# A gate's mask in the tile of the gates' sums, and the parts of paired token operands in another order

## The chip, the cores and the metric

The kernel runs on one core of a Trainium2 chip. Its time is the device time of one execution, in microseconds (us). The engines are named as in the profile: PE is TensorE (PEld its weight loads), DVE is VectorE, ACT is ScalarE, POOL is GpSimd, SP is SyncE, which here only issues DMAs. All engines run side by side, each through its own list of instructions in a fixed order; semaphores make one wait for another.

## The reference

Attention with mixed heads, and behind it a feed-forward whose gate is `h - tanh(h)`:

```python
# q, k, v: (8, 12, 448, 64)   w_pre, w_post: (12, 12)   w_in: (768, 2048)   w_out: (2048, 768)
scores = scale * np.matmul(q, k.transpose(0, 1, 3, 2))
scores = np.einsum('bhij,hg->bgij', scores, w_pre)
scores = scores - np.max(scores, axis=-1, keepdims=True)
attn = np.exp(scores)
attn = attn / (np.sum(attn, axis=-1, keepdims=True) + 1e-09)
attn = np.einsum('bhij,hg->bgij', attn, w_post)
x = np.matmul(attn, v).transpose(0, 2, 1, 3).reshape(3584, 768)
h = x @ w_in
g = h - np.tanh(h)
out = g @ w_out
```

## The kernel before

The first half, up to about 880 us, is the attention, batch by batch, with its output `xs` stored to DRAM. The change does not touch it. The second half is the feed-forward on 3584 tokens in seven blocks of 512 (`TB`). To keep fp32 precision, each operand is split into a high part (a copy rounded to a shorter type, on ACT) and a low part (the operand less its high part, on DVE), and each product is three matmuls: high by high, high by low, low by high.

**Block 0** is computed plainly. `Block0.step` is called 18 times, f = 0 to 17. Each of the first 16 makes one tile of 128 features of h in a PSUM bank, by 18 matmuls (lines 285, 286, 288), and copies the bank to SBUF (ACT, line 347). Every two steps one `Gate` is computed for two feature tiles.

**The gate.** `Gate` computes h − tanh(h) twice and picks one by a mask, so that small h keep their precision. On ACT: a1 (lines 301 and 302: u = h², and a square for a polynomial, into the work tile qa), a2 (line 306: tanh into t; line 307: another square into qb), a3 (line 317: the Relu of u − 0.25, which is the mask, over qb). On DVE: d1 (line 310 makes qa further, line 311 makes t = h − tanh h), d2 (line 314: qa from qb and qa), d3 (line 320: the polynomial's result into the tile ga or gb), d4 (line 323, copy_predicated: t over that result where the mask is not zero). The tiles u, qa, qb, t, ga, gb, gs and the two h tiles (h01, h23) come from a pool with one buffer for each tag: who writes a tag again waits for all that read or write it before, DMAs included.

**Three paired stages** follow, each on two blocks of tokens at once, by a scheme of seven products in place of eight (Strassen and Winograd). `pair_step` is called 8 times a stage (24 in all). Each step makes seven products of nine matmuls, in the order b11, b21, t2, t1, t3, b22, t4, where the names are those of the token operands: quarters of the two blocks' inputs (b11, b21, b22) or sums of quarters (t1 to t4). The products go in turn to two PSUM banks, X and Y. Of X, ACT empties the first result by line 677, before the third product (t2) overwrites X; others are emptied by lines 683, 692, 700, 704, 712 and 718. At the end of a step the first gate (g1) gets its a1, a2, d1, d2 and a3; its d3 and d4, and the whole second gate (g2), are done in the next step by `Late`, cut into v0 to v5 between the products. `Late` also makes the sums of gates that the second matmul wants: v4 allocates the tile gs (three planes of 512 tokens) and adds into it (line 652), v5 adds the third plane and one of gb (lines 655 and 656), and then POOL stores gb and gs to DRAM (lines 657 and 658; line 635 stores ga). Between these pieces stand units of `Results`, the second matmul: for these, stored gates are loaded again (gl), cast (ACT, line 437) and made into low parts (DVE, line 443), and lines 495 to 497 (block 0) and 525 to 527 (paired blocks) multiply them by w_out.

**The parts of the token operands** are made by `xq_jobs`, a generator of eleven jobs for a stage: `sub` is a DVE subtraction of a 128x1536 tile (line 565), `high` an ACT copy (line 569), `low` a DVE subtraction (line 572), `both` the last two of a quarter in place. All sums are made in the one tile xr. In block 0 `between0(f)` runs one job in each of the steps f = 6, 8 and 10 to 15; what is left goes into the first paired step, one job behind each product. Between stages the list `jobs` in the tail runs all eleven among units of the second matmul: 16 or 14 held back from the stage and 2 or 4 ahead.

**Order.** `in_order` fixes on each engine the order in which the program is written; no scheduler moves anything.

Of the kernel before, what the change touches and what calls it, by code (L numbers as in the profile page):

```python
# [12 lines left out]
I32 = mybir.dt.int32  # L13
U32 = mybir.dt.uint32
AF = mybir.ActivationFunctionType
# [6 lines left out]
def raw(ap):  # L22

    return ap.bitcast(F32)
# [126 lines left out]
def kernel_body(  # L151
# [11 lines left out]
    nc = tc.nc  # L163
# [15 lines left out]
    scale = 1.0 / float(D) ** 0.5  # L179
    NK = DM // P  # L180
    NF = DF // P
# [39 lines left out]
    ff = SimpleNamespace(w={}, x={}, xs={}, wa={}, w2={}, gr={}, gp={})  # L221

    def pool(name, bufs, side, stack=ctx):
        return stack.enter_context(tc.tile_pool(name=name, bufs=bufs, side=side, reuse_waits="tile"))
# [15 lines left out]
    def rest_of_line(stack):  # L240

        pad = stack.enter_context(tc.tile_pool(name="pad", bufs=1, side="right"))
        nc.gpsimd.memset(pad.tile([P, LINE - 8], F32, name="pad", tag="pad"), 0.0)

    def open_late():
        rest_of_line(ctx)
        ff.xqb, ff.ca = pool("xqb", 1, "right"), pool("ca", 3, "right")
        ff.ps_y = ctx.enter_context(tc.tile_pool(name="ps_y", bufs=1, space=PSUM, side="left"))
# [5 lines left out]
    def work(tag, n=2):  # L254
        return ff.rw.tile([P, n, TB], F32, name=tag, tag=tag)
# [38 lines left out]
    class Gate:  # L294
# [19 lines left out]
            nc.vector.scalar_tensor_tensor(out=self.qa, in0=self.qb, scalar=GATE_B[2], in1=self.qa, op0=ALU.add, op1=ALU.mult)  # L314

        def a3(self):
            nc.scalar.activation(self.qb, self.u, AF.Relu, bias=ff.bias[:, 2:3], scale=1.0)

        def d3(self, out):
            nc.vector.tensor_mul(out, self.qa, self.u)  # L320

        def d4(self, out):
            nc.vector.copy_predicated(out, self.qb.bitcast(I32), self.t)


    class Block0:
# [36 lines left out]
    class Results:  # L363
# [65 lines left out]
        def high(self, n):  # L429
            if self.n_high <= n < len(self.items):  # L430
                self.n_high += 1
                if self.lead and n % (len(IDLE) + 2) < len(IDLE):
                    hi = work(IDLE[n % (len(IDLE) + 2)]).bitcast(F32R)
                else:
                    hi = ff.gph.tile([P, 2, TB], F32R, name="gh", tag="gh")
                ff.gp[n] = hi, ff.gr.pop(n)
                nc.scalar.copy(hi, raw(ff.gp[n][1]))  # L437

        def low(self, n):
            if self.n_low <= n < len(self.items):  # L440
                self.n_low += 1
                hi, lo = ff.gp[n]
                nc.vector.tensor_sub(lo, raw(lo), raw(hi))  # L443
# [106 lines left out]
    def x_tiles(*names):  # L550
        for x in names:
            p = ff.xqa if x == "t4l" else ff.xqb
            ff.xs[x] = p.tile([P, HK, TB], F32R, name=x, tag=x)
# [8 lines left out]
    def xq_jobs():  # L562

        def sub(x, y):
            nc.vector.tensor_sub(xr, x if x is xr else raw(ff.xs[x]), y if y is xr else raw(ff.xs[y]))

        def high(x, src):
            x_tiles(x + "h")
            nc.scalar.copy(ff.xs[x + "h"], src)

        def low(x, src):
            nc.vector.tensor_sub(ff.xs[x + "l"], src, raw(ff.xs[x + "h"]))

        def both(x):
            high(x, raw(ff.xs[x + "l"]))
            low(x, raw(ff.xs[x + "l"]))

        xr = ff.xr.tile([P, HK, TB], F32, name="xr", tag="xr")
        sub("t3l", "b11l")
        yield  # L580
        both("b11")
        yield
        x_tiles("t1l")
        high("t1", xr)
        low("t1", xr)
        yield
        sub("b22l", xr)
        yield
        x_tiles("t2l")
        high("t2", xr)  # L590
        low("t2", xr)
        yield
        sub("b21l", xr)
        yield
        x_tiles("t4l")
        high("t4", xr)
        low("t4", xr)
        yield
        both("b21")
        yield  # L600
        sub("b22l", "t3l")
        yield
        high("t3", xr)
        low("t3", xr)
        yield
        both("b22")
        yield

    IDLE = ("u", "qa", "qb", "t", "h01", "h23")
# [114 lines left out]
    with ExitStack() as st:  # L724
# [295 lines left out]
        def now(*engines):  # L1020
            place[0] += 1
            engines = engines or (nc.sync,)
            for x in (queue, slow):
                while x:
                    send(x, engines[len(x) % len(engines)])
# [43 lines left out]
        for w in range(2):  # L1069
            for at in AT[w]:  # L1070
                x = repeat[:, w, at : at + HP].rearrange("p (i h) -> p i h", i=GH)
                nc.gpsimd.affine_select(
                    out=x, in_=x, compare_op=ALU.not_equal, fill=1.0, base=0, pattern=[[0, GH], [-1, H]],
# [4 lines left out]
        both = tmp_w[:, 2 * P : 2 * P + 4 * HP].rearrange("p (w a n) -> p w a n", w=2, a=2)  # L1078
        for w in range(2):
            for a in range(2):  # L1080
                if w == 0:
                    x = both[:, w, a].rearrange("p (i g) -> p i g", i=GH)
                    of, step = ps_w[:, w, :].unsqueeze(1).to_broadcast([P, GH, H]), [[H, GH], [0, H]]
                else:
                    x = both[:, w, a].rearrange("p (g i) -> p g i", i=GH)
# [4 lines left out]
                    out=x, in_=x, compare_op=ALU.is_ge, fill=0.0, base=-AT[w][a], pattern=[[-m, n] for m, n in step],  # L1090
# [3 lines left out]
                    out=x, in_=x, compare_op=ALU.is_ge, fill=0.0, base=AT[w][a] + H - 1, pattern=step,  # L1094
# [60 lines left out]
        while halved:  # L1155
            ready = sorted((x for x in halved if x[0] <= p), key=lambda x: (x[1], x[3:]))
            if ready:
                x = ready[0]
# [3 lines left out]
                if x[2] == kind and other and x[1] > p + 1:  # L1162
                    x = other[0]
                halved.remove(x)
                _, _, kind, i, n = x
# [58 lines left out]
        block0 = Block0()  # L1224
# [8 lines left out]
        for p in range(NPL + 3):  # L1233
# [39 lines left out]
                open_ps_h()  # L1273
            for f in start.get(p, ()):
                f()
        for _ in range(2):
            block0.step()
        now()


    open_late()
    xq = iter(())

    def xq_loads(s):
        ba, bb = 2 * s + 1, 2 * s + 2
        for x, b, h in (("b11l", ba, 0), ("b21l", ba, 1), ("t3l", bb, 0), ("b22l", bb, 1)):
            yield from load_xq(x, b, h)

    xq, xl = xq_jobs(), xq_loads(0)
    res = Results()  # L1290
    ff.n_wa, ff.stored = 0, [0] * NS

    def between0(f):
        if f >= 3:
            for _ in range(4 if f % 2 else 2):
                next(xl, None)
        if f in (10, 12):
            res.more_w2((f - 10) // 2)
        if f in (13, 15):
            res.more_gr((f - 13) // 2)  # L1300
        if 6 <= f < NF and f not in (7, 9):
            next(xq, None)

    while block0.f < NF + 2:
        block0.step(between0)
        if block0.f == NF:
            res.high(0)
            res.low(0)
# [4 lines left out]
    late, left = None, 4 * NQ  # L1313
    for s in range(NS):
        for p in range(NQ):

            def between(i):
                next(xq, None)
                if p == NQ - 1 and s + 1 < NS:
                    for _ in range((2, 2, 2, 0, 1, 3, 2)[i]):  # L1320
                        next(xl, None)

            if p == NQ - 1 and s + 1 < NS:
                xl = xq_loads(s + 1)
            many = FIRST[s] if p == 0 else (left - HELD[s] - FIRST[s]) * p // (NQ - 1) - (left - HELD[s] - FIRST[s]) * (p - 1) // (NQ - 1)
            late = pair_step(s, p, late, [many * (i + 1) // 7 - many * i // 7 for i in range(7)], between)
        left = 7 * NQ - AHEAD[s]
        if s + 1 < NS:
            xq = xq_jobs()
        else:  # L1330
            res.deepen()
        job = partial(next, xq, None)
        jobs = [
            [late.v0], [late.v1, late.v2], [late.v3], [late.v4], [late.v5, job], [job, job], [job, job], [job, job],
            [job, job], [job, job],
        ]
        n = HELD[s] + AHEAD[s]
        for i in range(0, n, 2):
            res.units(1)
            for f in jobs.pop(0) if jobs else ():  # L1340
                f()
            for _ in range(2):
                next(xl, None)
            res.units(1)
        for fs in jobs:
            for f in fs:
                f()
        late = None
# [33 lines left out]
```

## Time and profile before

| | us |
|---|---|
| median of 3 runs | 1755.94 (1752.22 to 1756.95) |
| profiled execution, its own time | 1768.5 |
| its span, first to last instruction | 1766.8 |
| attention, up to about | 880 |
| end of block 0 and start of the first paired stage | 897 to 981 |
| rest of the first paired stage | 981 to 1110 |
| second paired stage | 1186 to 1360 |
| passage to the third | 1360 to 1419 |
| third paired stage | 1419 to 1620 |

All stretches are of the profiled execution, which took 12.6 us longer than the median, so a sum made in it is scaled at its end. The granted TensorE clock of the profiled execution is 0.975 on average. A row of the timeline gives start, duration, engine, line, operation and tiles, and in brackets the idle time of the engine ahead of it with what released it. A row of waits gives engine, tile and line that waited, behind the arrow engine, tile and line waited for, then us in total, times, and the longest. Line numbers are those of the kernel before; from line 318 on they are greater by one after the change.

### The profile page before, as it was taken

Reading aid. Unit: us, or ns where it says so; the run is one execution under the profiler, and the core shown is the slowest. Engines: PE = TensorE matmul, PEld = TensorE weight load, DVE = VectorE, ACT = ScalarE, POOL = GpSimd, SP = SyncE. Lnnn points to the kernel's source line nnn. Section 1 sums busy time; section 2 is a strip of 40 time slices with the busy share of each in tenths; the row PEclk is TensorE's granted clock in tenths of the full one; section 3 lists DMA queues with packets and bytes.
Section 4 is the critical chain, followed back from the end, with each engine's and each line's share of the span. In section 5 each row is a group of like instructions: output and inputs, shape, how many; then the busy total and the mean of one; then the engine's idle time right before and its main releaser. Section 6 shows DMA issues by size and latency. Waiting matters only on the chain.

```text
span 1766.8 us, 41167 instructions
## 1 busy us (share of the span) xinstructions
PE 1692.2 (96%) x16068; PEld 1399.9 (79%) x16068; DVE 1232.0 (70%) x2119; ACT 1145.3 (65%) x2016; POOL 489.1 (28%) x702
## 2 busy tenths in 40 slices
PE   8999999999999999999997999899999799999999
PEld 6777777777777677777775788788888788989999
DVE  5676777766777767775368899668777767778432
ACT  5776777768878777876476677455666456666331
POOL 1355455555555545451100011011001101001000
PEclk9998999999999989999998999999999999999999
DMA  8778789788887978865497789989889879888994
GB/s 184 201 226 238 226 253 273 223 256 236 246 259 233 263 227 246 258 203 173 166 309 269 243 305 310 318 279 328 324 303 366 320 251 334 300 313 319 405 415 156
DMA packets 322289, 475.09 MB, mean 269 GB/s; under 512 B 105264, under 2 KB 255280, under 8 KB 322096
## 3 DMA queue, kind: packets, MB, share of 16 engines
q1 hardware_dynamic: 305660, 414.34, 73.0%
q0 software_dynamic: 16128, 57.68, 8.3%
q8 instruction: 128, 2.10, 0.5%
q14 instruction: 65, 0.53, 0.1%
q10 hardware_dynamic: 308, 0.43, 0.1%
HBM read 274.73 MB, written 120.59 MB: 224 GB/s over the span
## 4 chain that ended last, share of the span: by engine, by line
PE 77%; DMA 6%; ACT 6%; DVE 6%; issue 3%; SPq 1%; POOL 1%; DVEq 0%; ACTq 0%; POOLq 0%
PE ps_o L945 14%; PE ps_m L987 8%; PE ps_p L906 8%; PE ps_h L285 7%; PE ps_h L286 6%; PE ps_h L288 6%; PE ps_q L862 6%; PE y L527 6%; PE y L525 6%; PE y L526 6%; DMA vr<-in_v_dram 1%; PE ps_m L828 1%; DMA t3l<-xs 1%; ACT e L917 1%; ACT at L955 1%
## 5 line engine op out<-in xcount | busy, mean ns | idle before, releaser
L945 PEld LDWEIGHTS ps_o<-wr,e 60*112 60x112 f32 (+1 forms) x5760 | 308.0, 176 | 46.6 <-POOL wr L928 12.4
L945 PE MATMUL ps_o<-wr,e 60*112 60x60 f32 (+1 forms) x5760 | 317.7, 260 | 17.6 <-ACT at L955 12.3
L915 DVE TENSOR_REDUCE mx<-ps_p 128x1 f32<-128x448 f32 x360 | 207.2, 617 | 165.0 <-PE ps_p L906 164.8
L917 ACT ACTIVATE e<-ps_p,mx 128x448 f32<-128x448 f32 x360 | 225.7, 634 | 106.6 <-DVE mx L915 98.7
L955 ACT COPY at<-ps_o 112x960 f32<-112x960 f32 x156 | 153.7, 985 | 88.3 <-PE ps_o L945 87.6
L928 POOL TENSOR_TENSOR wr<-wpost,zs 128x120 f32<-128x120 f32 x180 | 69.8, 388 | 437.6 <-DVE zs L927 330.1
L906 PE MATMUL ps_p<-t,wpre 60*64 60x448 f32 (+1 forms) x1440 | 186.1, 585 | 4.7 <-DMA t<-s 3.5
L987 PEld LDWEIGHTS ps_m<-at,vr 112*64 112x64 f32 x3072 | 152.2, 140 | 29.2 <-ACT at L962 11.2
L987 PE MATMUL ps_m<-at,vr 112*64 112x120 f32 (+1 forms) x3072 | 166.7, 266 | 5.4 <-ACT at L962 3.1
L525 PE MATMUL y<-w,gh 128*128 128x384 f32 x448 | 153.7, 343 | 5.5 <-DMA w<-ts 3.7
L527 PE MATMUL y<-w,gl 128*128 128x384 f32 x424 | 145.7, 344 | 8.5 <-DVE gl L443 8.4
L526 PE MATMUL y<-w,gh 128*128 128x384 f32 x448 | 152.8, 341 | 0.0
L862 PEld LDWEIGHTS ps_q<-kk,qh 64*120 64x120 f32 (+1 forms) x768 | 62.0, 182 | 88.9 <-issue 61.8
L862 PE MATMUL ps_q<-kk,qh 64*120 64x448 f32 (+1 forms) x768 | 127.3, 408 | 2.2 <-DVE kk L814 1.4
L867 DVE COPY s<-ps_q 120x448 f32<-120x448 f32 (+1 forms) x192 | 112.9, 615 | 11.3 <-PE ps_q L862 11.1
L301 ACT ACTIVATE u<-h 128x1024 f32<-128x1024 f32 x56 | 59.5, 1062 | 67.4 <-DVE h L704 66.5
L867 ACT COPY s<-ps_q 120x448 f32<-120x448 f32 (+1 forms) x192 | 95.5, 539 | 7.0 <-PE ps_q L862 6.7
L657 POOL DMA_DIRECT2D gs<-gb x24 | 17.2, 718 | 297.7 <-DVE gb L656 282.1
L525 PEld LDWEIGHTS y<-w,gh 128*128 128x128 f32 x448 | 86.0, 192 | 11.2 <-ACT u L301 4.0
L437 ACT CAST gh<-gl 128x1024 fp32r<-128x1024 f32 x61 | 63.5, 1040 | 47.6 <-DMA gl<-gs 21.3
L527 PEld LDWEIGHTS y<-w,gl 128*128 128x128 f32 x424 | 81.4, 192 | 10.3 <-DVE gl L443 10.1
L526 PEld LDWEIGHTS y<-w,gh 128*128 128x128 f32 x448 | 85.9, 192 | 3.4
(370 smaller groups left out, 3895.5 us busy)
## 6 DMA issues: line engine op xcount, KB each, us to landing
t<-s SPq DMA_DIRECT2D x342, 210.0 KB
wa<-ss SPq DMA_DIRECT2D x96, 384.0 KB
w<-wo SPq DMA_DIRECT2D x43, 768.0 KB
gl<-gs SPq DMA_DIRECT2D x62, 512.0 KB
wa<-wi SPq DMA_DIRECT2D x72, 384.0 KB
w<-ts SPq DMA_DIRECT2D x35, 768.0 KB
gs<-gs POOLq DMA_DIRECT2D x24, 768.0 KB, 8.9
cr<-in_moe_w_in_dram SPq DMA_DIRECT2D x48, 256.0 KB
```

The lines of the kernel that those rows point to most:

```text
L285: nc.tensor.matmul(ph, w[:, c, 0], xh, start=start and c == 0, stop=False, skip_group_check=True)
L525: nc.tensor.matmul(y, gh[:, tok], wh, start=first, stop=False, skip_group_check=True)
L526: nc.tensor.matmul(y, gh[:, tok], wl, start=False, stop=False, skip_group_check=True)
L527: nc.tensor.matmul(y, gl[:, tok], wh, start=False, stop=last, skip_group_check=True)
L862: nc.tensor.matmul(ps[:n, :S], qx[a, hp, :], kx[a, hp % 2], start=(x == 0), stop=(x == 2))
L867: eng(sts[i][:n, 2 * hp + j, :], ps[:n, :S])
L906: nc.tensor.matmul(pss[r][halves[j], :], wpre[k, :], ts[j][k, :], start=True, stop=True)
L915: nc.vector.tensor_reduce(out=mx, in_=ps, axis=AX.X, op=ALU.max, negate=True)
L917: nc.scalar.activation(e, ps, AF.Exp, bias=mx, scale=1.0, accum_out=zs[:, 0, r : r + 1])
L945: nc.tensor.matmul(ps[:CP, j, c * GP : (c + 1) * GP].rearrange("p (h i) -> p h i", i=GI)[:, :, r * GH : (r + 1) * GH], e[k, c * CP : (c + ...
L955: nc.scalar.copy(ats[i0][:, :, :, at : at + 2 * GI].rearrange("p c h (j i) -> p j (c h) i", j=2), ps[:CP, :, : NC * GP].rearrange("p j (x ...
L987: nc.tensor.matmul(pv[j * D : (j + 1) * D, r, :n], vt[:, j, c, :], ats[i][:, c, 2 * hp + j, :n], start=(c == 0), stop=(c == NC - 1),)
```

## The change

Three edits. First, the gate's mask no longer goes over qb but into a tile of the tag gs, the tag of the sums of gates; d4 reads it there. Second, the eleven jobs on the operand parts are made in another order, with t3's sum made early and t2's made from it by adding b11, and b22 and t4 last; in block 0 they run in steps 6 to 8 and 10 to 15 (nine steps, not eight), and in the passages between stages the list has nine places for them, so that two go into the first step of the next stage. Third, block 0's third step stands behind the end of attention (`now()`, `open_late()`).

```diff
@@ class Gate
         def a3(self):
-            nc.scalar.activation(self.qb, self.u, AF.Relu, bias=ff.bias[:, 2:3], scale=1.0)
+            self.mk = work("gs", 3)[:, :2]
+            nc.scalar.activation(self.mk, self.u, AF.Relu, bias=ff.bias[:, 2:3], scale=1.0)
...
         def d4(self, out):
-            nc.vector.copy_predicated(out, self.qb.bitcast(I32), self.t)
+            nc.vector.copy_predicated(out, self.mk.bitcast(I32), self.t)
@@ xq_jobs
+        def parts(x):
+            high(x, xr)
+            low(x, xr)
+
         sub("t3l", "b11l")
+        yield
+        x_tiles("t1l")
+        parts("t1")
+        yield
+        sub("b22l", "t3l")
+        yield
+        parts("t3")
+        yield
+        nc.vector.tensor_add(xr, xr, raw(ff.xs["b11l"]))
         yield
         both("b11")
         yield
-        x_tiles("t1l")
-        high("t1", xr)
-        low("t1", xr)
-        yield
-        sub("b22l", xr)
-        yield
         x_tiles("t2l")
-        high("t2", xr)
-        low("t2", xr)
+        parts("t2")
         yield
         sub("b21l", xr)
         yield
-        x_tiles("t4l")
-        high("t4", xr)
-        low("t4", xr)
-        yield
         both("b21")
         yield
-        sub("b22l", "t3l")
+        both("b22")
         yield
-        high("t3", xr)
-        low("t3", xr)
-        yield
-        both("b22")
+        x_tiles("t4l")
+        parts("t4")
         yield
@@ end of attention
-        for _ in range(2):
-            block0.step()
+        block0.step()
         now()
 
     open_late()
+    block0.step()
@@ between0
-        if 6 <= f < NF and f not in (7, 9):
+        if f in (6, 7, 8, 10, 11, 12, 13, 14, 15):
             next(xq, None)
@@ tail of a stage
         jobs = [
-            [late.v0], [late.v1, late.v2], [late.v3], [late.v4], [late.v5, job], [job, job], [job, job], [job, job],
-            [job, job], [job, job],
+            [late.v0], [late.v1, late.v2], [late.v3], [late.v4], [late.v5, job], [job, job], [job, job], [job, job], [job, job],
         ]
```

Two places show how the instructions stand. On ACT, the end of a paired step of the first stage, from the tanh of the first gate to the start of the next gate; a row gives line, operation, tile written and read, size and what semaphores it waits on, where DMASW is a DMA issued by POOL and DMAHW one by SP. Before:

```order
L306 ACTIVATE t<-h_14146 128x1024
L307 ACTIVATE qb<-u,bias 128x1024
L718 COPY h_14185<-ps_h 128x512 [waits PE_49]
L317 ACTIVATE qb<-u,bias 128x1024 [waits DVE_49]
L437 CAST gh<-gl 128x1024 [waits DMAHW3_49]
L677 COPY h_14289<-ps_h 128x512 [waits PE_49]
L301 ACTIVATE u<-h_14185 128x1024 [waits DVE_49,Activation_49]
```

After:

```order
L306 ACTIVATE t<-h_14155 128x1024
L307 ACTIVATE qb<-u,bias 128x1024
L719 COPY h_14194<-ps_h 128x512 [waits PE_49]
L318 ACTIVATE gs<-u,bias 128x1024 [waits DMASW2_49,DVE_49]
L438 CAST gh<-gl 128x1024 [waits DMAHW3_49]
L678 COPY h_14300<-ps_h 128x512 [waits DVE_49,PE_49]
L301 ACTIVATE u<-h_14194 128x1024 [waits DVE_49,Activation_49]
```

The instructions stand in the same order. The Relu now writes gs and waits on a POOL DMA, the store of gs that the same step issued. It has such a wait in 23 of the 24 paired steps.

On DVE, the end of block 0, from the last low part of t4 before and the same place after; `b21l<-b21l,b21h` and the like are low parts, `xr<-` are sums. Before:

```order
L572 TENSOR_TENSOR b21l<-b21l,b21h 128x1536
L314 SCALAR_TENSOR_TENSOR qa<-qb,qa 128x1024
L320 TENSOR_TENSOR gb<-qa,u 128x1024
L323 COPY_PREDICATED gb<-qb,t 128x1024
L443 TENSOR_TENSOR gl<-gl,gh 128x1024
L310 SCALAR_TENSOR_TENSOR qa<-qa,h_13878 128x1024
L311 TENSOR_TENSOR t<-h_13878,t 128x1024
L314 SCALAR_TENSOR_TENSOR qa<-qb,qa 128x1024
L320 TENSOR_TENSOR ga<-qa,u 128x1024
L323 COPY_PREDICATED ga<-qb,t 128x1024
L565 TENSOR_TENSOR xr<-b22l,t3l 128x1536
L683 TENSOR_TENSOR h_13978<-ps_h,h_13978 128x512
```

After:

```order
L573 TENSOR_TENSOR b21l<-b21l,b21h 128x1536
L314 SCALAR_TENSOR_TENSOR qa<-qb,qa 128x1024
L321 TENSOR_TENSOR gb<-qa,u 128x1024
L324 COPY_PREDICATED gb<-gs,t 128x1024
L444 TENSOR_TENSOR gl<-gl,gh 128x1024
L310 SCALAR_TENSOR_TENSOR qa<-qa,h_13884 128x1024
L311 TENSOR_TENSOR t<-h_13884,t 128x1024
L314 SCALAR_TENSOR_TENSOR qa<-qb,qa 128x1024
L321 TENSOR_TENSOR ga<-qa,u 128x1024
L324 COPY_PREDICATED ga<-gs,t 128x1024
L573 TENSOR_TENSOR b22l<-b22l,b22h 128x1536
L684 TENSOR_TENSOR h_13986<-ps_h,h_13986 128x512
```

Around the last gates of block 0 the count of DVE's operations stays, and two operand jobs instead of three are left for the first paired step, whose first line is the last but one. PE's and POOL's orders are the same before and after; on SP one store of xs and one weight load change places at block 0's third step.

## The prediction

> **What bounds the kernel now.** I read the page's head first, then the chain of waits, then the busy time by stretches.
>
> ```profile
> span 1766.8 us, 41167 instructions
> PE 1692.2 (96%) x16068; PEld 1399.9 (79%) x16068; DVE 1232.0 (70%) x2119; ACT 1145.3 (65%) x2016; POOL 489.1 (28%) x702
> PE 77%; DMA 6%; ACT 6%; DVE 6%; issue 3%; SPq 1%; POOL 1%; DVEq 0%; ACTq 0%; POOLq 0%
> ```
>
> TensorE is busy for 96% of the span and makes up 77% of the chain: as a whole the kernel is bound by PE, and only 74.6 us of the span leave PE idle. The change touches only the feed-forward, the second half. The busy time of the five engines in its stretches (end of block 0 with the start of the first paired stage; the rest of the first paired stage; the second stage; the passage to the third; the third stage):
>
> ```profile
> core 0: us, PE busy (x) PEld busy (x) DVE busy (x) ACT busy (x) POOL busy (x), PEclk, DMA share, GB/s
> 897.00:981.00 84.00, 70.56 (x294) 55.34 (x293) 69.78 (x55) 58.72 (x63) 3.74 (x7) 0.94 0.80 281
> 981.00:1110.00 129.00, 126.55 (x584) 103.75 (x584) 116.90 (x114) 90.23 (x100) 15.29 (x21) 1.00 0.87 294
> 1186.00:1360.00 174.00, 173.49 (x853) 154.55 (x852) 137.61 (x134) 112.31 (x132) 19.65 (x29) 1.00 0.90 322
> 1360.00:1419.00 59.00, 45.64 (x219) 42.83 (x218) 40.48 (x37) 23.79 (x22) 6.54 (x11) 0.88 0.86 319
> 1419.00:1620.00 201.00, 201.00 (x992) 179.87 (x991) 147.28 (x143) 122.57 (x143) 19.62 (x29) 1.00 0.86 298
> ```
>
> Two things are to be seen. The first paired stage (second row) has PE at 98% and DVE at 116.90 of 129.00, 91%: a delay that DVE takes on there can be made up out of 12.1 us at most. The second and third stages have PE full and DVE at 79% and 73%. PE stands idle in only two places: 13.4 us in the first row, 13.4 us in the fourth.
>
> **What the mask's new tile removes.** The Relu that makes the mask (line 317) wrote over qb and so had to wait until DVE had read qb in line 314. That wait, and those around it at the end of block 0 (897 to 981 us):
>
> ```profile
> ACT qb L317 <- DVE qa L314: 35.8, 36, 2.8
> ...
> ACT qb L317 <- DVE qa L314: 14.2, 7, 2.8
> DVE qa L310 <- ACT qa L302: 6.6, 7, 1.8
> PE ps_h L285 <- ACT h L347: 5.0, 2, 3.6
> PE ps_h L285 <- ACT h L677: 3.8, 1, 3.8
> PE ps_h L286 <- DVE b21l L572: 0.6, 1, 0.6
> ...
> ACT qb L317 <- DVE qa L314: 9.5, 12, 1.1
> ```
>
> The first row is of the whole span, 35.8 us in 36 waits, and the last of the rest of the first paired stage (999 to 1109 us). They are ACT's, at 65% busy, so they count only where ACT is late for PE. At the end of block 0 it is: PE waits 5.0 us for ACT to empty a bank (line 347), 3.8 us for the same at line 677, and 0.6 us for a part. The most to be gained there is 9.4 us. But DVE is busy for 69.8 of the 84 us in that stretch, and the change moves one more part there, an operation of 1.75 us (below). ACT's freed wait helps DVE only by the 6.6 us that DVE waits for line 302. I take a third, **−3.5 us** (bounds 0 and −9.4).
>
> **What the new tile adds.** The tag gs has one buffer. In a paired step the same tile holds the sums that Late.v4 and v5 make and that POOL stores (line 658); at the end of the same step the mask of the new gate is written into it. So the Relu now waits until that store has landed: the order of instructions after shows this DMA wait on 23 Relus, seven in the first stage and eight in each of the others. Before, only line 652 of the next step had to wait for that landing. The end of a step of the first stage, from DVE, POOL, ACT and PE, and that step's store:
>
> ```profile
> 1088.08 0.69 DVE L656 TENSOR_TENSOR gb<-gb,gs 128x512 f32<-128x512 f32 x1
> 1089.77 0.76 POOL L658 DMA_DIRECT2D gs<-gs  x1
> gs<-gs POOLq DMA_DIRECT2D x1, 768.0 KB, 8.5
> 1093.28 1.15 ACT L317 ACTIVATE qb<-u,bias 128x1024 f32<-128x1024 f32 x1 [1.10 <-DVE qa L314]
> 1094.87 0.59 ACT L677 COPY h<-ps_h 128x512 f32<-128x512 f32 x1 [0.44 <-PE ps_h L288]
> 1095.62 1.40 DVE L323 COPY_PREDICATED ga<-qb,t 128x1024 f32<-128x1024 int32 x1
> 1096.71 0.39 PE L285 MATMUL ps_h<-t2h,wa 128*128 128x512 f32 x1
> ```
>
> The store is issued at 1089.77, 1.0 us after DVE's last sum (line 656) ends, and lands 8.5 us later, at 1098.3. The Relu starts at 1093.28, 3.5 us after the issue. Had it waited for the landing, it would have started 5.0 us late. Behind it on ACT stands line 677, which empties the bank that PE's third product (t2) writes: copied by 1095.46, used from 1096.71, a margin of 1.25 us. Behind the mask on DVE stands line 323, then the rest of DVE's queue, which has no slack here. All these are late by the wait. The stage's steps and stores:
>
> ```profile
> L656 DVE TENSOR_TENSOR gb<-gb,gs x7: 691/692/694, 995.4 to 1106.6; 128x512 f32<-128x512 f32 x7
> L658 POOL DMA_DIRECT2D gs<-gs x7: 752/752/764, 997.1 to 1108.3; - x7
> DMA to landing us min/median/max: 6.1/8.5/11.1
> ```
>
> A step takes (1106.6 − 995.4) / 6 = 18.5 us. From the Relu at 1093.28 to the end of the next line 656, at 1107.3, DVE works almost without a pause: 14.0 us. That makes a loop, with the landing as its new link: 14.0 us of work, 1.0 us to the issue, the landing, and the next Relu. With the median landing of 8.5 it is 23.5 us, 5.0 more than now; with the shortest, 6.1, it is 21.1, 2.6 more. A longer step carries the same bytes: the DMA engines' share of 0.87 goes to about 0.73 (0.87 × 18.5 / 22), so landings should be nearer the short end. I take 7.0: 22.0 us, 3.5 more. The seventh wait ends in the tail, where much else is ready for PE; six count: 6 × 3.5 = **+21 us** (bounds 6 × 2.6 = 15.6 less the 12.1 us that DVE could make up, so +3.5, and 6 × 5.0 = +30).
>
> [...]
>
> In the second and third stages steps are longer, and more stands between the Relu and PE. Their stores (second stage, third stage), then a step's end in the third:
>
> ```profile
> L658 POOL DMA_DIRECT2D gs<-gs x7: 750/752/764, 1204.4 to 1354.5; - x7
> DMA to landing us min/median/max: 6.6/7.7/10.5
> L658 POOL DMA_DIRECT2D gs<-gs x7: 750/752/769, 1462.0 to 1616.3; - x7
> DMA to landing us min/median/max: 6.3/11.2/11.6
> ...
> 1511.98 0.75 POOL L658 DMA_DIRECT2D gs<-gs  x1
> 1517.74 1.16 ACT L317 ACTIVATE qb<-u,bias 128x1024 f32<-128x1024 f32 x1
> 1521.44 0.59 ACT L677 COPY h<-ps_h 128x512 f32<-128x512 f32 x1 [1.03 <-PE ps_h L288]
> 1525.39 0.39 PE L285 MATMUL ps_h<-t2h,wa 128*128 128x512 f32 x1
> ```
>
> Here the Relu starts 5.8 us after the issue. With a landing of 7.7 it would be 1.9 us late, with 11.2 it would be 5.4 late. ACT has line 677 done at 1522.0, 3.4 us before PE's t2 needs the bank, and 1.0 us of its own waiting before that. So the median store of the second stage costs nothing, and that of the third up to 5.4 − 3.4 = 2.0 us. Bounds: 0, and eight of the third stage at 2.0 = +16. I take the middle, **+8 us**: PE is full here, so all that gets through counts.
>
> **The parts in another order.** The subtractions, additions, casts and low parts are as many as before (eleven jobs), each a row of 1.75 us on DVE or an equal copy on ACT. In block 0 nine instead of eight jobs run at steps 6 to 15, the other two in the first paired step, where b22 and t4 are wanted only by the sixth and seventh product. In a passage between stages two jobs move from the tail into the next first step in the same way. The tail's waits (1360 to 1420 us):
>
> ```profile
> PE y L527 <- DVE gl L443: 8.4, 4, 3.5
> PE y L525 <- DMA w<-ts: 3.7, 1, 3.7
> PE y L525 <- ACT t1h L569: 0.5, 1, 0.5
> ```
>
> PE waits 8.4 us for low parts of results (line 443), which stand in DVE's queue among the operand parts, and 3.7 us for weights, which the change doesn't touch. As the same number of operand parts stands ahead of most low parts, I expect a few short waits for casts to go, not the queue itself: **−2 us** (bounds 0 and −8.9). The moved jobs run in the first step, where DVE has 21 to 27% free. The exchange of a store and a weight load on SP at block 0's third step I cost at nothing: attention's last work covers both; uncovered it is one issue's time, under 1 us.
>
> **The sum.** The profiled execution took 1768.5 us with a span of 1766.8. 1768.5 − 3.5 + 21 + 8 − 2 = 1792.0, +1.3%. The runs' median, 1755.94, is 0.9929 of the profiled execution, so the forecast is 1792 × 0.9929 = **1779 us**.
>
> **The rivals.**
>
> *The store is not felt and the gains decide (faster).* The Relu comes 3.5 us after the issue; if the store lands within that, nothing is added and the two idle places of PE shrink. Full gains are −9.4 − 8.9 = −18, two thirds of it −12: 1756.5 × 0.9929 = **1744 us**. It decides from landings under about 4 us in the first stage. For it: a calmer DMA share after the stretch. Against it: 21 landings before, none under 6.1, at shares from 0.86 to 0.90. Chance 0.10. [...]
>
> *Loss and gain cancel (within 0.3%).* Landings stay at 6.1 and DVE makes up its 12.1 idle us: +3.5; the later stages cover their waits: 0; gains −3.5 − 2 and a little more. That is −2 to −5 on 1768.5, scaled **1753 us**. For it: the freed Relu also takes 9.5 us of waits from ACT in this very stage. Against: DVE's pauses lie at other points of the step than the wait. Chance 0.14.
>
> *It passes on in full (slower still).* Landings stay at 8.5 in the first stage (+30), the third stage pays 2.0 eight times (+16), and the operand order gains nothing, since DVE bounds both passages: +46, 1814.5 × 0.9929 = **1802 us**. For it: PE is full after 1186 us, and low parts (line 443) stand behind the mask too. Against: a slower step lightens the DMA engines. Chance 0.13.
>
> *The change doesn't do what it says:* the wait on line 314 goes, but as DVE is the later of the two, PE gains nothing at the end of block 0. That is the forecast with 3.5 us more, 1783, and lies in its range; it has no chance apart.
>
> **How the numbers follow.** The forecast has 0.63; its own range is the sum with each term moved halfway to its bounds, from 1768.5 + 12.2 + 4 − 12 to 1768.5 + 25.5 + 12 − 3, scaled 1760 to 1790. The range for 8 in 10 leaves out most of the first rival and part of the worst: **1754 to 1794**. A difference of under 0.3% (5.3 us) this kernel's measurement can hardly tell from none. Faster by more: 0.10; within: 0.14; slower: 0.76, the forecast and the worst case.
>
> **What the profile after would show.** The waits of the mask's Relu (line 318 then) on line 314 are gone, and in their place stand 23 waits for a DMA of gs, 3 to 5 us each in the first stage; line 656 there recurs every 22 us instead of 18.5; PE waits at line 285 for ACT's copy of line 678 by about that much per step. PE's waits of 5.0 and 3.8 us at the end of block 0 are shorter, those for gl in the passages a little. I am wrong if line 656 keeps its 18.5 us, that is if the stores land within 4 us or the Relu has no such wait; if the steps stretch but the time doesn't, the loss was given back in a place that I hold to be full.

## The result, and the profile after

| | median us | range | runs |
|---|---|---|---|
| before | 1756.45 | 1752.22 to 1759.91 | 4 |
| after | 1801.43 | 1793.18 to 1810.56 | 4 |

The ratio is 1.0258, with a 95% interval of 1.0202 to 1.0315: the change makes the kernel 45 us slower. The forecast was 1779, with a range of 1754 to 1794. The direction was right; the loss is twice what was forecast, and the time lies above the range.

The head of the page of the changed kernel, and two lines of its chain of waits, by engine and by line:

```profile
span 1802.2 us, 41206 instructions
PE 1691.4 (94%) x16068; PEld 1397.9 (78%) x16068; DVE 1230.2 (68%) x2119; ACT 1140.5 (63%) x2016; POOL 489.8 (27%) x702
PE 61%; DMA 16%; DVE 9%; ACT 7%; issue 5%; SPq 1%; POOL 1%; DVEq 0%; ACTq 0%; POOLq 0%
PE ps_o L946 13%; DMA gs<-gs 8%; PE ps_m L988 8%; PE ps_p L907 8%; PE ps_q L863 5%; PE y L528 4%; PE y L526 4%; PE y L527 4%; PE ps_h L285 4%; PE ps_h L286 3%; PE ps_h L288 3%; DMA t<-s 3%; PE ps_m L829 1%; DMA vr<-in_v_dram 1%; DVE qa L314
```

No engine has more work than before: the busy times differ by less than 5 us. What is new is in the chain. The store of gs, which did not appear in it, is 8% of it, about 149 us, and PE's share falls from 77% to 61%. (The 3% of t<-s are the attention's, which the change doesn't touch.) The table of waits over the whole span says where the store is waited for:

```profile
ACT gs L318 <- DMA gs<-gs: 116.6, 21, 9.7
DVE ga L324 <- ACT gs L318: 94.2, 21, 8.6
PE ps_h L285 <- ACT h L678: 28.7, 11, 7.6
```

The 35.8 us in which the mask's Relu waited for DVE are gone, and 116.6 us of waiting for a DMA have come, up to 9.7 us at a time. DVE waits for the mask in turn, 94.2 us, and PE for the bank that ACT empties behind the Relu. One step of the first stage, from POOL, ACT, DVE and PE:

```profile
1014.69 0.76 POOL L659 DMA_DIRECT2D gs<-gs  x1
1016.54 0.56 ACT L719 COPY h<-ps_h 128x512 f32<-128x512 f32 x1
1018.21 1.23 DVE L321 TENSOR_TENSOR ga<-qa,u 128x1024 f32<-128x1024 f32 x1
1024.38 1.15 ACT L318 ACTIVATE gs<-u,bias 128x1024 f32<-128x1024 f32 x1 [7.28 <-DMA gs<-gs]
1025.44 0.57 ACT L678 COPY h<-ps_h 128x512 f32<-128x512 f32 x1
1025.56 1.37 DVE L324 COPY_PREDICATED ga<-gs,t 128x1024 f32<-128x1024 int32 x1 [6.13 <-ACT gs L318]
1026.06 0.72 PE L285 MATMUL ps_h<-t2h,wa 128*128 128x512 f32 x1 [4.24 <-ACT h L678]
1028.70 1.26 PE L288 MATMUL ps_h<-t2h,wa 128*128 128x512 f32 x3
1029.81 0.39 PE L285 MATMUL ps_h<-t1h,wa 128*128 128x512 f32 x1
```

ACT is done with its other work at 1017.1 and sits until the store, issued at 1014.69, has landed at 1024.3. DVE has run out of work at 1019.4 and waits 6.13 us. PE waits 4.24 us for the copy behind the Relu. The stretches of the three stages, to be held against the rows of before:

```profile
core 0: us, PE busy (x) PEld busy (x) DVE busy (x) ACT busy (x) POOL busy (x), PEclk, DMA share, GB/s
973.00:1111.00 138.00, 114.62 (x502) 92.74 (x502) 99.25 (x97) 76.90 (x86) 13.13 (x18) 0.94 0.71 233
1177.00:1356.00 179.00, 176.21 (x863) 156.29 (x863) 132.97 (x128) 106.01 (x124) 15.30 (x22) 1.00 0.88 306
1438.00:1624.00 186.00, 179.27 (x876) 158.09 (x875) 131.93 (x128) 106.62 (x124) 15.30 (x22) 1.00 0.84 291
```

In the first stage PE is idle for 23.4 of 138 us, DVE's share has fallen from 91% to 72%, and the DMA engines' from 0.87 to 0.71. The next rows are the sums (line 657) of the first stage, and the stores of the first, the second and the third stage:

```profile
L657 DVE TENSOR_TENSOR gb<-gb,gs x7: 691/692/693, 986.8 to 1128.4; 128x512 f32<-128x512 f32 x7
L659 POOL DMA_DIRECT2D gs<-gs x7: 752/752/764, 988.6 to 1130.1; - x7
DMA to landing us min/median/max: 6.1/7.8/12.0
L659 POOL DMA_DIRECT2D gs<-gs x7: 752/752/764, 1222.2 to 1375.5; - x7
DMA to landing us min/median/max: 6.9/8.9/10.9
L659 POOL DMA_DIRECT2D gs<-gs x7: 752/752/772, 1480.5 to 1647.4; - x7
DMA to landing us min/median/max: 9.4/11.4/12.9
```

A step of the first stage takes (1128.4 − 986.8) / 6 = 23.6 us, where it took 18.5. The landings did not become shorter with the longer steps: the first stage's median is lower than before (7.8 against 8.5), but its mean is not (8.4 against 8.1), and the medians of the later stages, 8.9 and 11.4, are above the 7.7 and 11.2 of before.

For the rest of this text the time is cut by the starts of the first matmul of the first product (b11) in each paired step, read from the timelines, and by the first matmul of block 0. Each profiled execution reaches that matmul after an attention of its own length (855 to 868 us, with no change in the program there; before had 868.1, after 862.0), so the stages tell more than the spans. In us:

| kernel | block 0 and first step | first stage, 6 steps | its last step and passage | second stage, 7 steps | its last step and passage | third stage, 7 steps | last step and end | sum |
|---|---|---|---|---|---|---|---|---|
| before | 113.6 | 111.0 | 66.2 | 176.4 | 83.8 | 177.2 | 170.4 | 898.6 |
| after | 111.1 | 137.6 | 66.5 | 178.8 | 81.6 | 185.9 | 178.7 | 940.2 |
| e1, parts' order alone | 115.2 | 110.8 | 66.2 | 175.9 | 82.9 | 177.2 | 170.2 | 898.4 |
| e2, mask in gs alone | 111.0 | 135.8 | 67.6 | 179.7 | 84.2 | 184.0 | 176.0 | 938.3 |
| e3, mask in xr | 108.9 | 109.1 | 65.4 | 175.9 | 82.3 | 177.2 | 170.1 | 888.9 |
| e4, gs stored first | 110.0 | 122.8 | 67.1 | 175.8 | 83.4 | 177.2 | 172.8 | 909.1 |
| e5, mask in xr, old order | 111.4 | 109.2 | 65.5 | 176.4 | 84.3 | 177.2 | 170.3 | 894.3 |
| e6, half the weight tiles | 111.0 | 120.9 | 60.5 | 176.2 | 78.6 | 180.3 | 177.2 | 904.7 |
| e7, Relu behind the copy | 109.1 | 131.5 | 65.7 | 178.9 | 80.3 | 182.9 | 175.5 | 923.9 |
| e8, gs in the first stage | 108.6 | 136.9 | 67.3 | 175.8 | 81.0 | 177.2 | 172.2 | 919.0 |
| e9, gs in the other two | 110.1 | 109.1 | 67.7 | 178.9 | 81.5 | 184.2 | 177.7 | 909.2 |

From before to after the sum grows by 41.6 us; the medians say 45, with an interval of 35 to 55. Each row is one execution. How far to trust it can be seen where the mask isn't in gs: five kernels have 175.8 to 176.4 in the second stage, and all of them 177.2 in the third. Block 0 with the first step scatters more: the seven kernels with the new order and the mask out of qb have 108.6 to 111.1.

### The profile page after: what moved, and what is told of

It reads as the page before. It is cut to its first block, busy times and chain, and to the rows that moved or that the text cites. A ratio compares the mean times of both kernels' runs of the same rounds, so it can differ in the third digit from the quotient of the medians.

```text
span 1802.2 us, 41206 instructions
## 1 busy us (share of the span) xinstructions
PE 1691.4 (94%) x16068; PEld 1397.9 (78%) x16068; DVE 1230.2 (68%) x2119; ACT 1140.5 (63%) x2016; POOL 489.8 (27%) x702
## 4 chain that ended last, share of the span: by engine, by line
PE 61%; DMA 16%; DVE 9%; ACT 7%; issue 5%; SPq 1%; POOL 1%; DVEq 0%; ACTq 0%; POOLq 0%
PE ps_o L946 13%; DMA gs<-gs 8%; PE ps_m L988 8%; PE ps_p L907 8%; PE ps_q L863 5%; PE y L528 4%; PE y L526 4%; PE y L527 4%; PE ps_h L285 4%; PE ps_h L286 3%; PE ps_h L288 3%; DMA t<-s 3%; PE ps_m L829 1%; DMA vr<-in_v_dram 1%; DVE qa L314 1%
## 5 line engine op out<-in xcount | busy, mean ns | idle before, releaser
L907 PE MATMUL ps_p<-t,wpre 60*64 60x448 f32 (+1 forms) x1440 | 182.1, 573 | 8.2 <-DMA t<-s 7.2
L988 PEld LDWEIGHTS ps_m<-at,vr 112*64 112x64 f32 x3072 | 150.0, 138 | 30.8 <-ACT at L963 11.2
L318 ACT ACTIVATE gs<-u,bias 128x1024 f32<-128x1024 f32 x56 | 64.3, 1147 | 116.6 <-DMA gs<-gs 116.6
L301 ACT ACTIVATE u<-h 128x1024 f32<-128x1024 f32 x56 | 59.6, 1063 | 88.4 <-DVE h L705 83.8
L526 PEld LDWEIGHTS y<-w,gh 128*128 128x128 f32 x448 | 86.3, 193 | 22.8 <-issue 5.9
L324 DVE COPY_PREDICATED ga<-gs,t 128x1024 f32<-128x1024 int32 x28 | 38.8, 1385 | 94.9 <-ACT gs L318 94.2
L636 POOL DMA_DIRECT2D gs<-ga x24 | 17.2, 717 | 307.8 <-DVE ga L324 307.8
L528 PEld LDWEIGHTS y<-w,gl 128*128 128x128 f32 x424 | 81.5, 192 | 15.2 <-DVE gl L444 15.2
```

The lines of the kernel that those rows point to most:

```text
L526: nc.tensor.matmul(y, gh[:, tok], wh, start=first, stop=False, skip_group_check=True)
L528: nc.tensor.matmul(y, gl[:, tok], wh, start=False, stop=last, skip_group_check=True)
L907: nc.tensor.matmul(pss[r][halves[j], :], wpre[k, :], ts[j][k, :], start=True, stop=True)
L988: nc.tensor.matmul(pv[j * D : (j + 1) * D, r, :n], vt[:, j, c, :], ats[i][:, c, 2 * hp + j, :n], start=(c == 0), stop=(c == NC - 1),)
```

## The experiments

**Which edit costs.** First the parts' order alone, with the mask back in qb:

```diff
-            self.mk = work("gs", 3)[:, :2]
+            self.mk = self.qb
```

> The whole change, but the mask goes back over qb. Theory A (the Relu's wait for the landing of the store is the whole loss): no wait on a DMA of gs at the mask's Relu, line 657 recurs every 18.5 us in the first paired stage again, and the time is 2 to 6 us under before (1750 to 1755 us). Rival B (the parts' order, with b22 and t4 left to the first step, carries a part of the loss): 10 us or more over before, with PE waiting for operand parts in the first steps of the stages.

Measured: 1758.96 us against 1757.13, ratio 1.0013 (0.9990 to 1.0037). The wait for DVE is back as it was, and none for a store is left:

```profile
ACT qb L318 <- DVE qa L314: 36.2, 36, 3.0
```

Neither a loss of 10 us nor the expected gain of 2 to 6 can be seen: alone, the new order is worth nothing that this measurement finds. Then the other half, the kernel before with its mask in gs:

```diff
-            nc.scalar.activation(self.qb, self.u, AF.Relu, bias=ff.bias[:, 2:3], scale=1.0)
+            self.mk = work("gs", 3)[:, :2]
+            nc.scalar.activation(self.mk, self.u, AF.Relu, bias=ff.bias[:, 2:3], scale=1.0)
...
-            nc.vector.copy_predicated(out, self.qb.bitcast(I32), self.t)
+            nc.vector.copy_predicated(out, self.mk.bitcast(I32), self.t)
```

> The kernel before with only the mask moved into the tile of gs, parts in the old order. Theory A: about 45 to 50 us over before (1801 to 1806 us), the first paired stage longer by 27 us. Rival B: 25 us or less over before.

```profile
ACT gs L318 <- DMA gs<-gs: 106.0, 20, 8.8
```

Measured: 1798.90 us, ratio 1.0228 (1.0188 to 1.0269), 42 us over before; the first stage is 24.8 us longer. So the mask's tile is, within the noise, the whole loss, 3 us short of the 45 that were expected at least, and rival B falls.

**Is it the store, or any other tile?** In the paired steps the tile xr is idle once the operand parts are made. The mask goes there; in block 0 it stays in gs, which nothing stores at that time:

```diff
         def a3(self):
-            self.mk = work("gs", 3)[:, :2]
+            if self.paired:
+                self.mk = ff.xr.tile([P, HK, TB], F32, name="xr", tag="xr")[:, :2]
+            else:
+                self.mk = work("gs", 3)[:, :2]
...
-        g1 = Gate(h01)
+        g1 = Gate(h01, True)
...
-        return Late(s, q, g1, Gate(h23))
+        return Late(s, q, g1, Gate(h23, True))
```

> The whole change, but in the paired steps the mask goes into the tile xr, which is idle there once the parts are made; in block 0 it stays in gs, which nothing stores there. So the Relu waits neither for line 314 nor for a store. Theory A: no wait on a DMA of gs, and 3 to 9 us under before (1747 to 1754 us). Rival C (what costs is that the mask's readers are late, and that any second tile for the mask moves ACT ahead of DVE and brings other waits): 10 us or more over before.

The stretch of this kernel's first stage, which now takes 109 us over the same six steps:

```profile
971.00:1080.00 109.00, 107.66 (x500) 88.78 (x499) 99.82 (x98) 77.39 (x87) 13.12 (x18) 1.00 0.87 293
```

Measured: 1751.61 us, ratio 0.9971 (0.9949 to 0.9993). The Relu waits neither for line 314 nor for a store, PE is idle for 1.3 of 109 us, and the kernel is faster than both others, by 5.5 us than before. Rival C falls: a tile of its own costs nothing, the store does. Is the gain from the freed Relu or from the order? The same edit, made in the kernel before, with the parts in the old order:

> The kernel before with only the mask moved, into xr in the paired steps and into gs in block 0; the parts in the old order, three jobs left to the first step. If the parts' order gives nothing of its own, as its run alone (1.0013) says: 0.995 to 0.999 of before, as the mask in xr with the new order. If the two need each other (the freed Relu lets the new order use its slack): within 0.2% of before, 1754 to 1760 us.

Measured: 1754.23 us against 1757.60, ratio 0.9987 (0.9963 to 1.0012). It lies between, and its interval overlaps with the last one and with 1. By the stages, block 0 with the first step gains 2.2 us by the mask alone, loses 1.6 by the order alone (e1), and gains 4.7 by both. That points to the two needing each other, but the differences are as large as the spread between executions, so it stays open.

**What sets the landing?** The change with the two stores of a step exchanged:

```diff
-            nc.gpsimd.dma_start(gss[self.s][:, 2:4, self.q], self.gb)
             nc.gpsimd.dma_start(gss[self.s][:, 4:7, self.q], self.gs)
+            nc.gpsimd.dma_start(gss[self.s][:, 2:4, self.q], self.gb)
```

> The whole change, but POOL issues the store of gs ahead of the store of gb (768 KB ahead of 512 KB). Nothing else differs. Theory A with the landing set by the bytes that move at once: gs is issued 0.7 us earlier and lands in about 5 to 6 us instead of 8.4 in the first stage, so the Relu waits 1 to 2 us there instead of 5, and the time falls to 8 to 20 us over before (1764 to 1777 us). Rival D (the landing is a delay of the queue or of memory, not of the bytes ahead): the landing stays over 8 us, and the time falls by no more than 0.7 us a step, 15 us in all (1786 to 1801 us).

Its stores in the first stage, and the Relu's waits for them there:

```profile
L658 POOL DMA_DIRECT2D gs<-gs x7: 752/764/777, 985.6 to 1110.5; - x7
DMA to landing us min/median/max: 5.0/6.6/9.9
ACT gs L318 <- DMA gs<-gs: 23.6, 7, 6.2
```

Measured: 1772.45 us, ratio 1.0080 (1.0046 to 1.0114), two thirds of the loss gone. gs no longer waits for the last sum on gb, so it is issued 1.4 us earlier after that sum, more than the 0.7 that I had counted, and it lands after 7.1 us on average (median 6.6), not 5 to 6. Rival D allowed 1786 at the least, and falls.

What moved at the time of a store in the changed kernel: first between the issue of the store shown above and its landing, 1014.7 to 1024.3, with the packets, MB and share of the loads' queue (q1) and the stores' (q0), then from the landing before to that issue:

```profile
DMA packets 901, 3.24 MB, mean 338 GB/s; under 512 B 81, under 2 KB 81, under 8 KB 901
q1 hardware_dynamic: 549, 1.93, 65.3%
q0 software_dynamic: 352, 1.31, 33.3%
...
DMA packets 679, 1.98 MB, mean 120 GB/s; under 512 B 80, under 2 KB 80, under 8 KB 678
```

The store shares its 9.6 us with 1.93 MB of loads, at 338 GB/s; the other 16.6 us of the step move 120 GB/s. The traffic comes in a burst, and the store stands in it. To take loads away and nothing else, every second weight tile of the paired products served two products, so half of these loads were left out (and the kernel no longer computes the reference):

```diff
             q, name = ff.n_wa // 7 % NQ, WA[ff.n_wa % 7][0]
-            w = ff.wap.tile([P, HK, 2, P], F32R, name="wa", tag="wa")
+            if ff.n_wa % 2:
+                ff.wa[ff.n_wa] = ff.wa_last
+                ff.n_wa += 1
+                continue
+            ff.wa_last = w = ff.wap.tile([P, HK, 2, P], F32R, name="wa", tag="wa")
```

> The whole change, but only every second weight tile of the paired products is loaded and each serves two products (so the result is not the reference's); PE, ACT, DVE and POOL have the same instructions. Theory A with the landing set by what moves at once: about 0.6 of the 3.4 MB that move between the store's issue and its landing are gone, so landings in the first stage fall from 8.4 us on average to about 7, a step from 23 to about 21.5 us, and the time by 8 to 16 us (1785 to 1793 us). Rival D (the landing is fixed by the queue or by memory): landings stay at 8 us or more, the time within 5 us of the change (1796 to 1806 us).

Its stores in the first stage, and what moved during one of them, 1015.1 to 1019.9:

```profile
L663 POOL DMA_DIRECT2D gs<-gs x7: 750/750/764, 992.7 to 1115.1; - x7
DMA to landing us min/median/max: 4.7/5.0/8.0
...
DMA packets 367, 1.34 MB, mean 278 GB/s; under 512 B 39, under 2 KB 39, under 8 KB 367
q0 software_dynamic: 352, 1.31, 73.0%
q1 hardware_dynamic: 15, 0.02, 1.3%
```

Measured: 1767.81 us, ratio 1.0056 (1.0035 to 1.0077). I had expected landings near 7 us on average and a time from 1785; the seven have a mean of 5.8 and a median of 5.0, and the first stage falls from 137.6 to 120.9. For most of them nearly all loads beside them are gone and not half: of the seven, the five with 0.39 MB of loads or less between issue and landing take 4.7 to 6.1 us, the two with 1.24 and 1.53 MB take 8.0 and 7.2. Of the time's 34 us under the change, 9 are in the two passages, which have less to load and have nothing to do with the mask. The store's bytes are unchanged and its landing falls from a mean of 8.4 to 5.8, with the loads: so the loads beside it set most of what is above 5 us, and rival D falls again.

In the window shown, where the stores take 73.0% of the DMA engines' time and the loads 1.3%, gs lands 4.7 us after its issue; in the first stage of the changed kernel, where loads move beside them, the stores of gs take 6.1 to 12.0.

**By which way does the wait reach PE?** The Relu is issued on ACT behind the copy that empties bank X, so that copy no longer waits (nor does a cast of line 438, in steps that have one between the two):

```diff
         g1.d2()
-        g1.a3()
@@ Late.v0
             self.ga = work("ga")
+            self.g1.a3()
             self.g2.a1()
```

> The whole change, but the first gate's Relu is issued on ACT behind the copy that empties bank X, so the wait for the landing no longer holds up that copy; nothing else moves. Theory A, as predicted (a loop Relu, 14 us of work on DVE, sums, store, landing, Relu sets the first stage's step): the first stage stays near 22 us a step, only the later stages win, 1785 to 1797 us. Rival E (the loss goes by bank X alone: PE waits for the copy behind the Relu, and DVE can make up the rest): 1757 to 1772 us.

Waits from 980 to 1130 us in this kernel:

```profile
DVE ga L324 <- ACT gs L318: 29.6, 7, 6.4
ACT gs L318 <- DMA gs<-gs: 21.7, 7, 4.6
PE ps_h L285 <- DVE h L685: 16.4, 6, 4.3
```

Measured: 1780.99 us, ratio 1.0135 (1.0112 to 1.0158). PE no longer waits for ACT's copy, but now for line 685, DVE's next emptying of a bank, behind the mask's line 324. The first stage is 131.5 us, 21.9 a step, near the 22 that theory A expected of the loop through DVE; the copy's own share there is 6 us. In all it wins 20 us, more than the 4 to 16 expected, about 3 each in the third stage and at the end. So both ways exist, and in the first stage the one through DVE is the larger.

**Do the stages' losses add up?** The kernel of e3 with the mask in gs in the first stage alone, and in the other two alone (in `pair_step`; the diff is e8's, and e9 has `s == 0` in both places):

```diff
-        g1 = Gate(h01, True)
+        g1 = Gate(h01, s > 0)
...
-        return Late(s, q, g1, Gate(h23, True))
+        return Late(s, q, g1, Gate(h23, s > 0))
```

> The whole change, but the mask goes into gs in block 0 and the first paired stage only; in the other two stages it goes into xr. If the losses of the stages stand by themselves: the first stage as long as with the whole change (137 us over seven step starts against 111), the others as in the kernel with xr alone, so about 27 us over that kernel: 1775 to 1783 us. If the first stage's loss is partly given back later (loads that come earlier, a fuller store of gates): under 1770 us.

> The other half: the mask in xr in the first paired stage, in gs in the second and the third. If the losses stand by themselves, the traces' sum for these stages and the tail is 3 + 9 + 8 = 20 us over the kernel with xr alone: 1767 to 1776 us. By the prediction's +8 for them: 1757 to 1763 us.

Waits for the store over the whole span, e8 and then e9; then all waits of PE in the third stage of the changed kernel (1437.6 to 1623.5), and PE's largest wait in its end, with what DVE did ahead of it (1658 to 1663):

```profile
ACT gs L321 <- DMA gs<-gs: 42.7, 7, 9.0
...
ACT gs L321 <- DMA gs<-gs: 72.3, 14, 8.1
...
PE y L528 <- DVE gl L444: 3.4, 3, 2.1
PE ps_h L285 <- ACT h L678: 2.7, 2, 1.6
PE y L526 <- ACT c L536: 0.6, 1, 0.6
...
1659.52 1.37 DVE L324 COPY_PREDICATED ga<-gs,t 128x1024 f32<-128x1024 int32 x1 [4.72 <-ACT gs L318]
1661.90 1.96 DVE L545 TENSOR_TENSOR c<-y,c 128x384 f32<-128x384 f32 x4
1662.56 0.66 PE L526 MATMUL y<-w,gh 128*128 128x384 f32 x1 [3.71 <-ACT qa L302]
```

Measured: e8 1779.02 us, ratio 1.0116 (1.0074 to 1.0158); e9 1768.29 us, ratio 1.0058 (1.0032 to 1.0084). Over e3 (1751.61, of another group of runs) that is 27.4 and 16.7 us, together 44.1; the whole change has 49.8 over e3. By the sums of the table, which leave the attention out, it is 30.1 and 20.3, together 50.4, against 51.3. Nothing is given back.

In the second stage PE waits for 2.8 us, and for no low part. In the third it waits 3.4 us for low parts of results (line 444), which stand on DVE behind the mask's copy_predicated, and 2.7 for the copy of line 678; before, it waited for nothing there. The other 2.0 of this stage's 8.7 us are a longer busy time of PE.

In the end PE's wait of 3.71 us is put down to ACT's line 302, which happens to end at 1662.56. But PE's queue was held until 1662.51 by a semaphore that DVE raises, and the first of the four operations of DVE's line 545, which empty the banks that PE's second matmul writes next, ends at 1662.46. They stand behind line 324, which waited for the mask. e9 has the same wait, 3.46 us. So in the end, too, the wait reaches PE through DVE. PE is idle for 10.4 us there, where it was for 5.5 before, and busy for 3.3 us longer.

## Why the prediction was right or wrong

**What bounds the kernel, and where the mask goes: right.** The Relu waits for the store of its own step, the wait holds up ACT's copy and DVE's line 324, and both reach PE. e2 and e3 show that this store is the whole loss. The waits for line 314 are gone, as predicted. Of the 23 waits that the order of instructions allowed, 21 are felt, in the first stage 3.8 to 9.7 us each where I had 3 to 5.

**End of block 0, −3.5: right.** Measured −2.5, within the bounds, in a stretch that scatters by as much. PE's waits of 5.0 and 3.8 us became 2.4 and 1.3, and one of 2.8 for line 684 came.

**First stage, +21: too small; measured +26.6.** The loop was right: from a Relu to the end of the next line 657 it takes, in the step shown, 1024.38 to 1038.3 (its next start, 1037.6, and 0.69), that is 13.9 us where I said 14.0; and one more us to the issue. What failed is the step "a longer step carries the same bytes … so landings should be nearer the short end", from which I took 7.0. The DMA engines' mean share did fall, to 0.71, as I had worked out; but the seven landings have a mean of 8.4, as those of before had 8.1 (58.7 and 57.0 us over seven, read one by one from the traces). A mean share says nothing of the burst in which the store stands: 338 GB/s beside it and 120 in the rest of the step. With 8.4 the same loop gives 23.4 us a step and +29, and 26.6 came.

**Second and third stages, +8: too small, and the largest miss.** Measured +2.4 in the second, +8.7 in the third, and +8.3 in the last step and the end, where the third stage's eighth wait lies: 19.4 us. The step that failed is "I take the middle": no row stood behind it. The median landing of 11.2 us in the third stage was in the profile, and with it the prediction's own bound for eight waits was +16; +17.0 came there. That this is so near is in part luck, since the margin of 3.4 us was reckoned for the bank alone. The bank made PE wait for only 2.7 us in the third stage. Low parts behind the mask, which the prediction named only for the worst case, made it wait for 3.4, and in the end it was line 545 on DVE, behind the same mask, that held it for 3.7; I had written only of the tail after the first stage. A further 2.0 us of the third stage and 3.3 of the end are a PE that is busy longer for the same work; for the third stage the reason isn't shown.

**The parts' order, −2: right in size, but not shown to be its own.** The second passage is 2.2 us shorter, the first 0.3 longer, each with its stage's last step. Alone the order gives 1.0013 (0.9990 to 1.0037).

**The rivals.** The worst case, 1802 us with a chance of 0.13, is the time that came. Its mechanism came in the main: landings stay near 8.5, and the third stage pays. That the number fits so well is partly luck: it has +46, made of +30, where 26.6 came, and +16, where 17.0 came by other ways than the bank, and neither the second stage's 2.4 nor the gains in block 0 and the second passage. Its third part, that the passages gain nothing, did not come. The case in which the store isn't felt had no support: no landing in the first stage was under 6.1 us. That DVE could make up 12.1 us, as in the middle rival, was not seen: its work in the loop takes what it took, and it only waits longer in the place before line 324.

**The sum.** −2.5 + 26.6 + 0.3 + 2.4 − 2.2 + 8.7 + 8.3 = +41.6 us in the stages, where I had +23.5. Of the 18.1 us between, 11.4 are in the later stages with the end, 5.6 in the first stage, and 1.0 in block 0: nearly all is the price of one wait in its different places.

## What to carry to other kernels

In this kernel a tile that a DMA read came free only at the landing, in the first stage 6.1 to 12.0 us after the issue; before a second use is found for such a tile, follow the new writer's wait up to the landing, and close the loop: what the delayed writer feeds, and when that issues the next DMA. Take the landing from the rows of the same stage, and don't shorten it by a mean DMA share (here the share fell from 0.87 to 0.71, and the mean landing went from 8.1 to 8.4): look at what moves in the store's own few microseconds. A tile whose last reader is an engine's instruction was at hand here, and with it the same idea gained 0.3% instead of losing 2.6%.

## What the runs showed of the hardware that I had not expected

Behind four pauses of PE, of 3.71 to 7.60 us, its granted clock was 0.50 to 0.54. The stretches behind one of them, the 4.24 us pause shown above (the columns as before):

```profile
1026.00:1028.00 2.00, 1.94 (x5) 1.58 (x6) 1.50 (x2) 1.97 (x3) 0.71 (x1) 0.54 0.00 0
1028.00:1030.00 2.00, 2.00 (x7) 1.58 (x6) 1.83 (x2) 2.00 (x3) 0.00 (x0) 0.60 0.69 262
1030.00:1032.00 2.00, 2.00 (x10) 1.61 (x9) 1.97 (x3) 1.50 (x3) 0.00 (x0) 1.00 0.49 106
```

The clock is 0.54 for the nine matmuls of t2, which take from 1026.06 to 1029.81, that is 3.75 us where the same product took 2.05 in the step shown of before (1096.71 to 1098.8); then it is full again. Over the first stage PE is busy for 114.62 us in the change, at a granted clock of 0.94, and for 107.66 in e3, at 1.00, for the same work: 7 us of the loss show as a slower PE, not as an idle one. Behind the pause of 3.71 us in the end the clock was 0.50 for about 5 us, from 1662.56 to 1667.9, and 1.00 after that. Behind a pause of 2.87 us, which ended at 1096.12, it was 1.00. What decides it, these runs don't settle.
